# Filler matmuls at the opening, mirrored rows by indexed DMA, and a re-ordered plan in a fused long-convolution and FFN kernel

## The chip, the cores and the metric

The kernel runs on one core of one Trainium2 chip. A core has TensorE (PE), VectorE (DVE), ScalarE (ACT), GpSimd (POOL) and SyncE (SP); SP, ACT and POOL also issue DMAs. The metric is the time of one execution on the device in microseconds (us); of several executions the median counts. A profile is taken of one execution. Its span goes from the first to the last instruction.

## The reference

Two halves work on a sequence of S = 2048 rows with D = 640 columns. The first is a long convolution with a gate, the second an FFN with F = 1728.

```python
k_shift = sum over t of k_pad[:, t:t + S, :] * shift_k[:, 3 - t]     # 4 taps
kv = k_shift * v
y = irfft(rfft(kv, 2S) * rfft(ssm_k, 2S))[:S] + kv * ssm_D           # along the rows
h = x + layernorm(x) * y                                             # x is A_q
h2 = h + (silu(g(h) @ w_gate) * (g(h) @ w_up)) @ w_down              # g is layernorm
```

Inputs and output are bf16.

## The kernel before

The sequence is cut into four blocks of 512 rows, a block into four row tiles of 128. The convolution is done blockwise with cosine and sine transforms of length 1024 as matmuls against constant bases: `g_transform(p)` transforms piece p of the convolution's kernel (eight tiles of 128 frequencies, the cosine half "c" and the sine half "s"), `hbuild` adds neighbouring pieces, `front(n)` makes kv of block n, and `x_transform(n)` its transform. `pair(j, p)` multiplies the transform of block j with that of piece p as complex numbers and adds it to the sum of block j + p: these are the DVE's long instructions, 128 x 2560 elements each (L453). `inverse(n)` brings the sum of block n back (L550), `ln` forms layer-norm statistics (ACT at L520 and L521, or `bn_stats` on the DVE at L516, then two tiny POOL instructions, L524 and L525), and `ffn(n)` does gate and up (L618), the product tT = silu(gate) * up (L632) and the down projection (L644), whose result is added to x on the DVE (L652) and stored.

The transforms use a symmetry: the first 256 rows of a block are needed in reversed order. So `front` mirrors two row tiles of kv on PE by a matmul with a reversed identity (L429), and `inverse` yields the even part es and the odd part os of half a block: their sum is the upper row tile (L566, L567), their difference, mirrored on PE by four matmuls (L574), the lower one, which the DVE reads from PSUM (L577). The normalised rows hl (L532) go transposed to hT by a DMA (L582), which the FFN reads.

The order of all work is computed on the host. Each call of `plan.add` gives an engine, an assumed duration, what is read and written, a priority `pr` and an earliest time `t0`. `Plan.order` simulates the engines with these, three times forward and backward (`ROUNDS = 3`), and keeps the best; the instructions are then issued in that order, and each engine executes its own in order. So SP's queue carries all loads of k, v, x, gate and up weights, the transposes and the stores in one fixed sequence, and one that waits holds back all behind it. PSUM has four buffers: psA0 and psA1 for the convolution, psF0 and psF1 for the kernel transforms and the FFN. The down weights wd are loaded by one DMA of 2,080 KB and one of 80 KB; until then the tile wd holds the transposed kernel pieces 0 to 2, and the first transpose passes through the tile tT (`kch`). F = 1728 is 13 chunks of 128 and a last one of 64, so the last pair of matmuls of each down tile has 64 rows. The first block's conv products come from k loaded once (`front_first`, L395, and banded matmuls, L405); w4, the four taps over all partitions, is made by PE and ACT (L347, L349).

Of the kernel before, what the change touches and what calls it, by code (L numbers as in the profile page):

```python
# [16 lines left out]
D = 640  # L17
# [37 lines left out]
class Plan:  # L55
# [3 lines left out]
    def __init__(self, pools):  # L59
        self.ops, self.writer, self.readers = [], {}, {}  # L60
        self.pools, self.held = pools, {}

    def add(self, eng, dur, fn, r=(), w=(), pr=0, acq=None, rel=None, kb=0, after=(), t0=0.0):
# [8 lines left out]
        i = len(self.ops)  # L72
        self.ops.append(dict(eng=eng, dur=dur, fn=fn, deps=deps, pr=pr, acq=acq and acq[0], rel=rel and rel[0], group=(acq or rel or (0, 0))[1], kb=kb, w=list(w), t0=t0))
# [117 lines left out]
ROUNDS = 3  # L191
# [3 lines left out]
MOVE = "add"  # L195
RES, XACT, VEC, TRANS = (), (), True, {2: 28, 3: 28}
# [11 lines left out]
def kernel(  # L208
# [33 lines left out]
    WI_h = nc.inline_tensor(make_basis()[2], name="const_wi")  # L242
    J_h = nc.inline_tensor(make_flip(), name="const_flip")
# [16 lines left out]
    kch = [tT[:, 2560 * i:2560 * (i + 1)].rearrange("p (a b) -> p a b", a=5) for i in range(2)]  # L260
# [21 lines left out]
    junk = tl("junk", [P, D])  # L282
    mhalf = tl("mhalf", [P, 1], FP32)
# [9 lines left out]
    gT = [wd[:, 0:4, :], wd[:, 4:8, :], wd[:, 8:12, :], hT[1][:].rearrange("p a b -> p (a b)").rearrange("p (a b) -> p a b", a=4)]  # L293

# [14 lines left out]

    def load(q, dst, src, w, pr, kb, r=(), dur=0.45, after=(), t0=0.0):  # L310
# [3 lines left out]

    add("POOL", 0.1, lambda: nc.gpsimd.memset(ones[:], 1.0), w=["ones"], pr=-99)
# [4 lines left out]

    def gload(p, pr, q="SP"):
# [5 lines left out]
        for kt in range(4):  # L327
            g = ("F", "T", p, kt)

            def mm(g=g, kt=kt):  # L330
# [6 lines left out]
            add("PE", 0.45, mm, r=["flip", f"kch{p % 2}"] + (["drow"] if p == 0 and kt == 0 else []), w=[g], pr=pr + 50, acq=("F", g))  # L337
            add("ACT", act(D), lambda g=g, kt=kt: nc.scalar.copy(gT[p][:, kt, :], ps(g).rearrange("p a b -> p (a b)")[:, 0:D]),  # L338
                r=[g], w=[f"gT{p}"], pr=pr - 40, rel=("F", g))
# [11 lines left out]
    for t in range(4):  # L351
        wcast(t)

    def g_transform(p, pr):
        for ct in range(NCT):
            g = ("F", "G", p, ct)

            def mm(g=g, ct=ct):
                for kt in range(4):
                    for h in range(2):  # L360
                        nc.tensor.matmul(ps(g)[:, h, 0:NH], WG[:, kt, ct * P:(ct + 1) * P],  # L361
                                         gT[p][:, kt, h * NH:(h + 1) * NH], start=(kt == 0), stop=(kt == 3))
            add("PE", 8 * 0.137, mm, r=["WG0", "WG1", f"gT{p}"], w=[g], pr=pr, acq=("F", g))
            add("ACT", act(D), lambda g=g, ct=ct: nc.scalar.copy(r3(G[p][ct // 4][:, ct % 4, :]), ps(g)[:, :, 0:NH]),  # L364
                r=[g], w=[Gk[p] + "cs"[ct // 4]], pr=pr - 900, rel=("F", g))
# [4 lines left out]

# [358 lines left out]
```

## Time and profile before

| What | Value |
|---|---|
| median of 8 runs | 296.18 us (294.76 to 297.66) |
| the profiled execution | 297.77 us, its span 296.0 us |
| busy PE / DVE / ACT / POOL | 275.7 / 229.8 / 169.7 / 65.8 us |
| first matmul of the first block's conv (L405) | 10.67 us |
| first y of block 0 on the DVE (L566) | 49.15 us |
| last long DVE instruction of block 3 ends | 227.65 us |
| gate and up of block 3 begin | 247.1 us |
| its down projection begins, last add begins | 276.25, 292.39 us |

A line of the page's second part cuts the span into 40 slices of 7.4 us and gives the busy share of each in tenths. In the chain, each row is a start, a length and what ran; the chain is followed back from the last instruction, at each step to what released it. "Busy" of PE is modelled, and matmuls overlap: 379 ns is the length of a 512-column matmul in the records, but they follow one another at 217 ns; those of 320 columns follow at 136 ns.

### The profile page before, as it was taken

The page shows a single profiled execution, that of the slowest core. Times are in us where ns is not written, and L with a number is a line of the kernel's source. Part 1 is how long each engine was busy: PE and PEld are TensorE (multiplying, and loading weights), DVE is VectorE, ACT ScalarE, POOL GpSimd, SP SyncE. Part 2 cuts the span into 40 slices and gives each one's busy share as a digit, 9 for nine tenths or more (in the row PEclk, how much of TensorE's full clock was granted, in tenths as well). Part 3 has the DMA queues.
Part 4 walks back from the last instruction along what each step waited for, and adds up shares of the span by engine and source line. Part 5 has one row for each costly group of instructions (what it writes and reads, how often), then busy time and mean ns, then how long its engine had stood idle before and what let it go on. Part 6 is the DMA issues. An engine that isn't in the chain of part 4 may idle for free.

```text
span 296.0 us, 4391 instructions
## 1 busy us (share of the span) xinstructions
PE 275.7 (93%) x1636; PEld 158.4 (54%) x1651; DVE 229.8 (78%) x301; ACT 169.7 (57%) x323; POOL 65.8 (22%) x70
## 2 busy tenths in 40 slices
PE   3598969999999989999999999999998999999995
PEld 1366646666645534664545555555444665444563
DVE  0649797999999999999999999999999931221211
ACT  5106896798765588104996790169955732555300
POOL 0000163295000046000353174008810210000000
PEclk9999999999999999999999999999999999999999
DMA  7982399607635587943676294163554152654011
GB/s 225 394 276 82 101 205 355 161 3 216 240 89 133 143 267 146 256 145 89 187 238 200 66 194 96 44 200 91 146 124 111 43 121 59 175 143 105 0 46 46
DMA packets 67898, 44.13 MB, mean 149 GB/s; under 512 B 25442, under 2 KB 65955, under 8 KB 67748
## 3 DMA queue, kind: packets, MB, share of 16 engines
q1 hardware_dynamic: 66240, 40.23, 50.2%
q10 hardware_dynamic: 1636, 3.61, 3.5%
q8 instruction: 13, 0.21, 0.3%
q14 instruction: 9, 0.07, 0.1%
HBM read 37.28 MB, written 2.62 MB: 135 GB/s over the span
## 4 chain that ended last, share of the span: by engine, by line
DVE 51%; PE 31%; DMA 7%; issue 4%; ACT 2%; POOL 2%; ACTq 0%; SPq 0%; DVEq 0%
DVE s L453 20%; DVE T L453 13%; PE psF L644 11%; PE psF L618 11%; DVE k L378 3%; DVE tT L632 3%; PE psA L405 3%; DMA perm<-const_flip 3%; DMA wu<-in_B_w_up_dram 2%; PE psF L361 2%; DVE k L379 2%; PE psA L550 2%; PE psA L443 2%; DMA hT<-hl 1%; DVE o L652 1%
## 5 line engine op out<-in xcount | busy, mean ns | idle before, releaser
L618 PE MATMUL psF<-hT,wg 128*128 128x512 bf16 x273 | 69.0, 379 | 1.3 <-ACT uc L630 0.8
L524 POOL TENSOR_SCALAR sm<-sm 128x1 f32<-128x1 f32 x32 | 30.3, 946 | 171.1 <-ACT junk L521 160.6
L644 PE MATMUL psF<-wd,tT 128*128 128x320 bf16 x448 | 64.8, 299 | 0.5 <-DVE tT L632 0.4
L618 PE MATMUL psF<-hT,wu 128*128 128x512 bf16 x252 | 63.0, 379 | 1.3 <-DMA wu<-in_B_w_up_dram 0.9
L623 ACT ACTIVATE sg<-psF 128x512 bf16<-128x512 f32 (+1 forms) x56 | 33.7, 602 | 45.0 <-PE psF L618 35.8
L644 PEld LDWEIGHTS <-tT 128*128 128x128 bf16 x448 | 41.4, 97 | 23.5 <-issue 6.9
L453 DVE TENSOR_TENSOR T<-s,s 128x2560 bf16<-128x2560 bf16 x32 | 47.4, 1485 | 0.0
L453 DVE TENSOR_TENSOR s<-s,T 128x2560 bf16<-128x2560 bf16 x32 | 47.2, 1484 | 0.0
L618 PEld LDWEIGHTS <-wg 128*128 128x128 bf16 x280 | 27.2, 98 | 32.7 <-issue 2.3
L630 ACT CAST uc<-psF 128x512 bf16<-128x512 f32 (+1 forms) x56 | 33.2, 592 | 16.3 <-PE psF L618 16.1
L632 DVE TENSOR_TENSOR tT<-sg,uc 128x512 bf16<-128x512 bf16 (+1 forms) x56 | 23.5, 423 | 24.3 <-ACT uc L630 24.3
L618 PEld LDWEIGHTS <-wu 128*128 128x128 bf16 x260 | 25.4, 98 | 30.1 <-DMA wu<-in_B_w_up_dram 1.4
L525 POOL TENSOR_TENSOR sm<-sm,mhalf 128x1 f32<-128x1 f32 x32 | 35.1, 1098 | 2.7
L361 PEld LDWEIGHTS <-s 128*128 128x128 bf16 x256 | 25.0, 98 | 11.8 <-issue 2.1
L361 PE MATMUL psF<-wd,s 128*128 128x320 bf16 x192 | 28.4, 299 | 0.9 <-ACT wd L338 0.5
L652 DVE TENSOR_TENSOR o<-psF,x 128x640 bf16<-128x640 f32 x16 | 13.1, 816 | 19.3 <-PE psF L644 19.3
L364 ACT CAST s<-psF 128x640 bf16<-128x640 f32 x32 | 21.8, 693 | 7.7 <-PE psF L361 7.6
L521 ACT ACTIVATE junk<-x,sm 128x640 bf16<-128x640 bf16 x28 | 23.7, 847 | 0.3
L520 ACT ACTIVATE junk<-x 128x640 bf16<-128x640 bf16 x28 | 20.9, 746 | 3.7 <-DVE x L578 2.9
L550 PE MATMUL psA<-s,WI 128*128 128x320 bf16 x128 | 18.9, 299 | 2.9 <-DVE s L453 2.8
L453 DVE TENSOR_TENSOR s<-s,s 128x2560 bf16<-128x2560 bf16 x14 | 20.5, 1482 | 1.2 <-ACT s L364 1.2
L443 PE MATMUL psA<-kv,WX 128*128 128x320 bf16 x128 | 20.5, 299 | 0.0
(55 smaller groups left out, 234.0 us busy)
## 6 DMA issues: line engine op xcount, KB each, us to landing
k<-in_A_k_dram SPq DMA_DIRECT2D x12, 640.0 KB, 4.9
wg<-in_B_w_gate_dram SPq DMA_DIRECT2D x24, 320.0 KB, 3.2
wu<-in_B_w_up_dram SPq DMA_DIRECT2D x24, 320.0 KB, 3.7
out_dram<-o SPq DMA_DIRECT2D x16, 160.0 KB, 1.9
wd<-in_B_w_down_dram SPq DMA_DIRECT2D x1, 2080.0 KB, 10.6
v<-in_A_v_dram SPq DMA_DIRECT2D x12, 160.0 KB, 4.7
x<-in_A_q_dram SPq DMA_DIRECT2D x3, 640.0 KB, 5.4
tT<-in_A_ssm_k_dram SPq DMA_DIRECT2D x2, 640.0 KB, 8.7
```

What stands on the lines that cost most here:

```text
L361: nc.tensor.matmul(ps(g)[:, h, 0:NH], WG[:, kt, ct * P:(ct + 1) * P], gT[p][:, kt, h * NH:(h + 1) * NH], start=(kt == 0), stop=(kt == 3))
L443: nc.tensor.matmul(ps(g)[:, h, 0:NH], WX[:, kt, ct * P:(ct + 1) * P], kv[:, base + kt, h * NH:(h + 1) * NH], start=(kt == 0), stop=(kt == 1))
L453: add("DVE", dve(n * D), lambda: f(o, a, b), r=ks(ak) + ks(bk), w=ks(ok), after=["WG0", "WG1"] if ok[:2] == "s7" else [], pr=pr)
L521: add("ACT", act(D) + 0.45, lambda: nc.scalar.activation(junk[:], src, ACT.Square, bias=s[:, 0:1], accum_out=s[:, 1:2]), r=[xk, k + "a"], ...
L524: e.tensor_scalar(s[:, 3:4], s[:, 1:2], 1.0 if vec else 1.0 / D, EPS, op0=ALU.mult, op1=ALU.add)
L525: e.tensor_tensor(s[:, 4:5], s[:, 3:4], mhalf[:], op=ALU.pow)
L550: nc.tensor.matmul(ps(g)[:, h, 0:NH], WI[:, 4 * part + ct, m * P:(m + 1) * P], a[part][:, ct, h * NH:(h + 1) * NH], start=(ct == 0), stop= ...
L618: i = nc.tensor.matmul(ps(gr)[:, which, :], w[:, kt, cc * P:(cc + 1) * P], hT[b][:, kt, :], start=(kt == 0), stop=(kt == 4))
L623: apart(gr, 0, nc.scalar.activation(sg[s][:z, :], ps(gr)[:z, 0, :], ACT.Silu))
L630: add("ACT", act(MB), lambda gr=gr, s=s, z=z, merged=merged: nc.scalar.copy(uc[s][:z, :], ps(gr)[64:128, 0, :] if merged else ps(gr)[:, 1, ...
L632: add("DVE", dve(MB), lambda c=c, s=s, z=z: TM(tT[:z, c * MB:(c + 1) * MB], sg[s][:z, :], uc[s][:z, :]), r=[f"sg{s}", f"uc{s}"], w=[f"tT{c ...
L644: nc.tensor.matmul(ps(gr)[:, h, 0:NH], tT[:z, c * MB + m * P:c * MB + (m + 1) * P], wd[:z, c, h * NH:(h + 1) * NH], start=(c == 0 and n no ...
```

## The change

- *Fillers.* A tile `junk` is zeroed by the DVE, and PE multiplies it with itself: five matmuls of 512 columns at the start and seven after the broadcast of the taps. The results are not used; a one-element DVE copy after each group releases the PSUM buffer.
- *Zero-padded last chunk.* The lower 64 rows of the last chunk of tT and wd are zeroed once, and the last pair of down matmuls has 128 rows.
- *Down weights.* Four loads (chunks 0 to 3, 4 to 7, 8 to 11, 12) and the one of 80 KB are placed among the gate and up loads of block 0.
- *Mirrored rows.* The lower row tiles 0 and 1 of each x block are gathered row by row in reversed order by an indirect DMA that POOL issues, are kept reversed throughout, and are scattered back to their places by an indirect DMA from POOL at the end. The difference es - os is then formed by the DVE from SBUF, and the L574 matmuls are gone. kv is still mirrored on PE.
- *Transposes.* In blocks 0 and 3 hl is transposed by PE and copied by ACT instead of by DMA (`TURN`).
- *Residual.* In block 2 x is added by two more matmuls per down tile with the identity, and ACT copies the result (`RES`).
- *Statistics.* Row tiles 2 and 3 of block 3 get `bn_stats` on the DVE; block 0 has them for all four as before (`VEC`).
- *Plan.* Named stages get offsets to their priorities (`URGENCY`) and earliest times (`EARLIEST`); the plan is one forward pass (`ROUNDS = 0`). The second buffer of `kch` lies elsewhere in tT, and `hbuild` stands at other places. The order of every engine changes.

```diff
+        i, pr = len(self.ops), pr + URGENCY.get(self.stage, 0)
+        t0 = max(t0, EARLIEST.get(self.stage, 0))
...
-ROUNDS = 3
+URGENCY = {"down 0": 4045, "front 3": -988, "front_first 2": 435, "front_first 3": 3649, "front_tile 3 0": -700, "g_transform 2": 562,
...
+EARLIEST = {"front 2": 89, "front_tile 1 1": 22, "front_tile 2 3": 96, "front_tile 3 0": 153, "g_transform 1": 34, "g_transform 2": 42,
...
+ROUNDS = 0
-MOVE = "add"
-RES, XACT, VEC, TRANS = (), (), True, {2: 28, 3: 28}
+RES = (2,)
+VEC = [(0, q) for q in range(4)] + [(3, 2), (3, 3)]
+TURN = (0, 3)
+GATHER = True
+WARM = (0.3, 5, 7)
...
+    rows = MB * np.arange(NB)[None, :, None] + P * np.arange(2)[None, None, :] + P - 1 - np.arange(P)[:, None, None]
+    idx_h = nc.inline_tensor(np.ascontiguousarray(rows.reshape(P, 2 * NB), dtype=np.int32), name="const_idx")
...
-    kch = [tT[:, 2560 * i:2560 * (i + 1)].rearrange("p (a b) -> p a b", a=5) for i in range(2)]
+    kch = [t.rearrange("p (a b) -> p a b", a=5) for t in (tT[:, 0:2560], tT[:, 8 * MB:13 * MB])]
...
+    add("DVE", 0.35, lambda: nc.vector.memset(junk[:], 0.0), w=["junk"], pr=-999)
+    add("DVE", 0.35, lambda: nc.vector.memset(tT[64:128, 13 * MB:], 0.0), w=["tz"], pr=-998)
+    add("DVE", 0.35, lambda: nc.vector.memset(wd[64:128, 13, :], 0.0), w=["wz"], pr=-998)
+    def warm(name, n, pr, r=()):
+        g = ("F", name)
+        def mm():
+            for i in range(n):
+                nc.tensor.matmul(ps(g)[:, i % 2, :], junk[:, 0:P], junk[:, 0:MB], start=True, stop=True)
+        add("PE", n * WARM[0], mm, r=["junk", *r], w=[g], pr=pr, acq=("F", g))
+        add("DVE", 0.1, lambda: nc.vector.tensor_copy(junk[0:1, 0:1], ps(g)[0:1, 0, 0:1]), r=[g], w=["junk"], pr=pr, rel=("F", g))
+    if WARM[1]:
+        warm("a", WARM[1], -300)
...
+    if WARM[2]:
+        warm("b", WARM[2], -70, r=[("A", "w", 3)])
...
+    def mirror(n, q):
+        return bass.IndirectOffsetOnAxis(ap=idx[:, 2 * n + q:2 * n + q + 1], axis=0)
...
+            load(queue, x[:, 2:4, :], xq[n * MB + 256:(n + 1) * MB, :].rearrange("(m p) d -> p m d", p=P), [f"x{n % 2}_{q}" for q in (2, 3)], pr, 320, t0=(14, 30, 0, 0)[n])
+            for q in (1, 0):
+                add("POOL", 1.2, lambda q=q: nc.gpsimd.indirect_dma_start(out=x[:, q, :], out_offset=None, in_=xq[:, :], in_offset=mirror(n, q), bounds_check=S_TOT - 1,
+                                                                      oob_is_err=False), r=["idx"], w=[f"x{n % 2}_{q}"], pr=pr, kb=160, t0=(14, 30, 0, 0)[n])
...
-                if half == 0:
-                    add("DVE", dve(D), lambda m=m, yb=yb: TA(yb[:], es[m][:], os_[m][:]), r=[f"eo0{m}", f"eo1{m}"], w=[yk], pr=pr)
+                if half == 0 or GATHER:
+                    add("DVE", dve(D), lambda m=m, yb=yb, f=(TA, TS)[half]: f(yb[:], es[m][:], os_[m][:]), r=[f"eo0{m}", f"eo1{m}"], w=[yk], pr=pr)
...
+                if n in TURN:
+                    g = ("A", "Q", n, q)
+                    def mm(g=g, half=half):
+                        flat = ps(g).rearrange("p a b -> p (a b)")
+                        for c in range(5):
+                            nc.tensor.matmul(flat[:, c * P:(c + 1) * P], hl[half][:, c * P:(c + 1) * P], ident, start=True, stop=True)
+                    add("PE", 0.5, mm, r=["flip", hk], w=[g], pr=pr, acq=("A", g))
...
-                        z = 64 if c == 13 else P
                         for h in range(2):
-                            nc.tensor.matmul(ps(gr)[:, h, 0:NH], tT[:z, c * MB + m * P:c * MB + (m + 1) * P],
-                                             wd[:z, c, h * NH:(h + 1) * NH], start=(c == 0 and n not in RES), stop=(c == 13))
+                            nc.tensor.matmul(ps(gr)[:, h, 0:NH], tT[:, c * MB + m * P:c * MB + (m + 1) * P],
+                                             wd[:, c, h * NH:(h + 1) * NH], start=(c == 0 and n not in RES), stop=(c == 13))
...
+            if m < 2 and GATHER:
+                add("POOL", 1.2, lambda m=m, s=s: nc.gpsimd.indirect_dma_start(out=oo[:, :], out_offset=mirror(n, m), in_=ot[s][:], in_offset=None), r=["idx", f"o{s}"], pr=pr - 300, kb=160)
+            else:
+                load("SP", oo[r0:r0 + P, :], ot[s][:], [], pr - 300, 160, r=[f"o{s}"])
...
+    wds = [(0, 4), (4, 8), (8, 12), (12, 13)]
+    def down_loads():
+        for i, (c0, c1) in enumerate(wds):
+            load("SP", wd[:, c0:c1, :], B_w_down[c0 * P:c1 * P, :].rearrange("(kt p) d -> p kt d", p=P), [f"wd{i}"], 1200, 160 * (c1 - c0),
+                 r=[f"tT{2 * min(i, 2) + 1}"], after=["gT0", "gT1", "gT2"])
...
-    load("SP", wd[:, 0:13, :], B_w_down[0:13 * P, :].rearrange("(kt p) d -> p kt d", p=P), ["wdl"], 1200, 2080, after=["gT0", "gT1", "gT2"], t0=40)
```

## The prediction

> **What bounds the kernel now.** I read the page's busy shares, then the chain of work that ended last in order of time (start, duration, what), then busy time by stage, then the timeline at the places that the change touches.
>
> ```profile
> PE 275.7 (93%) x1636; PEld 158.4 (54%) x1651; DVE 229.8 (78%) x301; ACT 169.7 (57%) x323; POOL 65.8 (22%) x70
> DVE  0649797999999999999999999999999931221211
> ```
>
> ```profile
> 10.67 2.31 PE psA L405 x8
> 12.98 1.07 PE psF L413 x4
> 14.05 4.99 PE psA L405 x28
> 20.53 2.01 PE psA L405 x14
> ...
> 49.15 0.50 DVE y L566
> ...
> 227.79 2.35 PE psA L550 x16
> 230.14 0.54 PE psA L574 x4
> 230.68 1.09 PE psF L644 x8
> 231.77 0.54 PE psA L574 x4
> 232.31 14.86 PE psF L644 x104
> 247.54 10.74 PE psF L618 x49
> ```
>
> Stages (stretch; its length; busy us of PE, PEld, DVE, ACT, POOL; clock; DMA share; GB/s):
>
> ```profile
> 60.00:225.00 165.00, 160.62 (x918) 89.23 (x928) 164.01 (x198) 106.01 (x210) 51.48 (x42) 1.00 0.57 152
> 227.75:247.10 19.35, 19.31 (x137) 12.64 (x137) 11.00 (x23) 9.56 (x20) 2.99 (x8) 1.00 0.38 94
> ```
>
> The shares name PE, but there are three stages. Up to 25 us loads and PE set the pace. From 60 to 225 us the DVE works 164.0 of 165.0 us: it is the bound. Its last sum for block 3 ends at 227.65 us (call this E). From there PE works alone: 19.45 us of inverse, mirroring and block 2's down projection until block 3's FFN starts at 247.1, then 29.15 us of gate and up, 16.1 of down, 3.6 of last add and store. A gain must come from E or from these 68.3 us. The profiled execution took 297.77 us, its span 296.0; the median shown is 1.6 us under it. I work out a difference within the span and take it from 296.18.
>
> **The change part by part.**
>
> *Fillers.* By the chain, L405 comes at 289 ns, L413 at 268, and at 20.53 L405 at 144, although the granted clock reads 1.00; the slow stretch lasts from 10.67 to about 15.4. Twelve fillers of 512 columns go ahead, five at the start and seven after the broadcast of the taps. At twice the warm 217 ns of L618 they take 2.2 and 3.0 us. The taps' matmuls end at 6.8; one more load issue (0.35) ahead of ACT's table load, and the first fillers, move that to about 7.5, so fillers run until 10.5. The first product, 0.6 later than now, is ready at 9.7; the 0.8 us between lies before today's 10.67. The slow stretch falls on fillers, and PE wins some 2.5 us. The new order spends them on earlier transposes of the first kernel chunk; the conv result that the DVE waits for at 22.58 comes at the same time. Bounds: 2.5 gained, 1 lost if the fillers run late.
> The Trainium skill, "TensorE: Matmul & The Clock Gate", Part 1, says that about 3.4 us of sustained work lifts the array from half to full rate; the row shows about 4.7. By 3.4 the opening would gain 0.6 us more.
>
> *Reordering.* The DVE now stands 1.72 us before the y at 49.15, waiting for the inverse. After, three conv steps (1.40 + 0.74 + 0.40) stand there and the first inverse's two parts are adjacent on PE. Against that, half of the first kernel transform comes later on PE, behind twenty transposes. I take -1.5 us; bounds -4 and +1. From there to E both kernels have the same 2560-element multiplies and sums of 1.40 us (94 in all before E), so the middle can't shrink.
>
> *Mirrored rows.* PE loses 32 L574 matmuls (0.54 per four, 4.4 us). On the DVE six PSUM reads of 0.73 before E become twelve ops of 0.40: +0.4. Other queues: SP loses eight stores, half of each x load and the eight transposes of blocks 0 and 3, which go to PE and ACT under other work. POOL, in order, gets eight gathers and eight stores, and SP's store of row tile 2 now waits for POOL's two to land. Behind it on SP stand an x load and weights; four chunks (about 11 us of PE with the x transform between) are loaded by then. On POOL the next block's statistics stand behind: they have 25 us in block 0 and 12.6 in block 1, against 3g + 4.
> This g, a DMA issued by POOL, no row shows. I bound it by SP's issue, 0.33 to 0.45 us, and POOL's longest instruction:
>
> ```profile
> 200.78 5.97 POOL L524 TENSOR_SCALAR sm<-sm 128x1 f32<-128x1 f32 x1 [19.71 <-ACT junk L521]
> 233.87 0.19 POOL L524 TENSOR_SCALAR sm<-sm 128x1 f32<-128x1 f32 x1 [18.29 <-ACT junk L521]
> ```
>
> The same instruction takes 0.19 us beside an idle DVE and up to 5.97 beside a full one. The means, 0.95 (L524) and 1.10 (L525), add to 2.0; I take g = 2.0, as an issue is several accesses like those. Where it hurts: row tile 0's output buffer is reused for tile 2, tile 1's for tile 3. In block 0 the new DVE order has 9.2 us of other work between the adds of tiles 1 and 2, and POOL needs two gathers, a store and its landing (1.9, the output row): 3g + 1.9. In block 1 it is 2g + 1.9 against 6.5 for tile 3. Both fit up to g = 2.3. At g = 3 the DVE loses 1.7 + 1.4 = 3.1 us, at 4, 8.1, at 6, 18. I add 0.5.
> The Trainium skill, "SBUF — State Buffer", under "SBUF: two separate sides", speaks against this part: descriptor writing by POOL is locked out by the DVE's two-port modes, 620 ns becoming 3100. No row here shows it; as an estimate, g = 3.1 would cost 3.6 us and put the forecast 3 us higher. The page's "Who interferes with whom" would spare tensor_tensor, by inference.
>
> *Down projection ahead of the inverse.* E is about 227.65 - 1.5 + 0.4 + 0.5 = 227.1. The new PE order puts 48 of block 2's 120 down matmuls (eight of them the new residual) and half of block 3's inverse before the last sum. From the last add of block 1 to E the DVE has 25 x 1.40 + 14 x 0.335 + 3.0 = 42.8 us; PE has 135 x 0.217 + 96 x 0.136 = 42.3 and starts about 1 us earlier. It fits, barely.
> After E: 8 down and 8 inverse matmuls, the os copy, at E + 2.55 the y (now E + 2.2); 13 DVE ops of 0.36 to 0.40, E + 7.65; statistics of tile 2 on the DVE (1.05), a scale, a sum, statistics of tile 3 (1.05), E + 10.5. Meanwhile tile 0's statistics on ACT (1.95) and POOL (0.85), E + 12.5; its scale 0.45, PE transpose 0.2 + 0.44 (the row of L334), ACT copy 0.2 + 0.69: the FFN starts at E + 14.8. PE's own work is 88 x 0.136 + 4 x 0.44 = 13.7, so the chain decides. Now it is E + 19.45: -4.7 us. Without the 48, PE needs E + 20.2: +0.8. The cover of the statistics gets 6.5 us thinner; what is late next is tile 0's.
>
> *Zero padding.* The switch to 64 rows leaves a gap in the weight loads, and so does the switch back:
>
> ```profile
> 238.70 0.11 PEld L644 LDWEIGHTS <-tT 64*128 64x128 bf16 x2 [0.26 <-issue]
> 239.07 3.37 PEld L644 LDWEIGHTS <-tT 128*128 128x128 bf16 x26 [0.26 <-issue]
> ```
>
> Twenty-eight take 4.01 us from 235.06 to 239.07, and 3.80 at 0.136. Four tiles in the last block: -0.9; the other twelve lie under the DVE. The memsets fall in the DVE's first 7.58 idle us.
>
> *Down weights.* One load of 2,080 KB becomes four beside the gate and up loads. A wait of PE for wu (0.94 at 110.74) can go, but the DVE was all but full: 0, bounds -0.4 (the DVE's idle there) and 0.
>
> Sum: -1.5 + 0.4 + 0.5 - 4.7 - 0.9 = -6.2 us; 290.0.
>
> **Rivals.**
> 1. *PE is not ahead at E* (a late weight load, or psF held by a late DVE op). For it: PE is busy 43.6 of 45 us from 180 to 225. Against: at full rate its work from 25 to 227.75 is 405 x 0.217 + 756 x 0.136 + 1.8 = 192.5 of 202.7 us, and about 198 after. The tail is 5.4 us longer: 295.4, no change.
> 2. *POOL's issues hold the output buffers.* In blocks 0 and 1 the DVE waits before an output add. Slower begins where the stalls reach 8.2 us, g = 4.0; g = 5 costs 13.1: 302.6. For it: POOL ops of 2.4, 3.5 and 5.97 us. Against: 36 of 64 take under 0.8.
> 3. *The opening gains all it can*: -4 in place of -1.5, no stall: 287.0.
>
> **How the numbers follow.** Forecast 0.53 (own range 287.5 to 293.0, from -4 to +1 at the opening and g up to 3); rival 1 0.16; rival 2 0.15; rival 3 0.16. A measurement of this kernel can tell about 0.5%, 1.5 us: under 294.7 is faster, over 297.7 slower. The forecast, rival 3 and a quarter of rival 1 are faster, 0.73; the rest of rival 1 is 0.10 the same and 0.02 slower, with rival 2 0.17. The range takes in rivals 1 and 3 and the first part of rival 2: 285.5 to 298.5.
>
> **What would show it.** Right: matmuls at 0.14 us by 12 us; the first y of block 0 near 47; E near 227; block 3's FFN some 15 us after E, with PE idle 1 to 2 us before it; no 64-row gaps; POOL issues near 2 us. Wrong: the DVE idle before an output add, ended by a DMA (rival 2), or gate and up matmuls of block 2 after E (rival 1). The weakest step is E: the order of 300 DVE instructions is redone, and any that waits for PE or ACT adds its wait whole.

## The result and the profile after

The changed kernel takes 298.1 us in the median of 20 executions (296.86 to 303.89), beside 297.04 us of the kernel before (294.76 to 300.11). The ratio is 1.0057, with a 95% interval from 1.0036 to 1.0079: slower by about half a per cent, where the prediction said 290.0 us and a chance of 0.17 for slower. The times of the changed kernel spread widely, and the profiled execution, at 302.82 us and a span of 301.0, is one of the long ones; ratios leave out executions more than 1.5% above the fastest of their kernel, so some of its long ones are not in them (below, three of eight are out in e5 and three of twelve in e14, which lowers those ratios).

From the page of the changed kernel, the span, the busy shares, and the rows by slices of 7.5 us (busy tenths of DVE and POOL, granted clock of PE):

```profile
span 301.0 us, 4515 instructions
## 1 busy us (share of the span) xinstructions
PE 278.2 (92%) x1664; PEld 162.0 (54%) x1679; DVE 230.8 (77%) x316; ACT 177.2 (59%) x327; POOL 114.5 (38%) x86
...
DVE  1757899999999999939999999878999792121221
...
POOL 0220580679997025964500458823000532000020
PEclk9999999999999999998999999959999999999999
```

The DVE's work has hardly changed (230.8 us, before 229.8), but its row is no longer a row of nines: it drops to 3 in one slice, 128 to 135 us, and to 8, 7 and 8 from 188 to 211. POOL's busy time went from 65.8 to 114.5 us. PE idled there too, and its clock row drops just after the first place and inside the second. Busy time by stage shows how much (stretch; its length; busy us of PE, PEld, DVE, ACT, POOL; clock; DMA share; GB/s):

```profile
125.00:135.00 10.00, 5.12 (x36) 3.45 (x34) 5.45 (x5) 4.37 (x9) 7.49 (x3) 0.96 0.21 59
...
190.00:205.00 15.00, 11.34 (x39) 4.42 (x38) 11.04 (x15) 8.46 (x19) 6.64 (x7) 0.77 0.39 112
205.00:235.00 30.00, 29.84 (x167) 16.40 (x168) 29.97 (x31) 17.78 (x31) 3.77 (x3) 1.00 0.47 121
```

Of the 25 us in the first two stretches the DVE works 16.5 and stands 8.5. After both, PE is granted a lower clock (0.77 over the second stretch). The third row is what the rest of the middle looks like: 29.97 of 30.

Both ends of the kernel came as predicted. The chain of work that ended last, at the opening and from the last long sum of block 3 (which ends at 238.28 us, E in the prediction) to the end:

```profile
6.97 3.10 PE psF L351 x7
...
10.78 1.42 PE psA L456 x8
...
13.97 2.01 PE psA L456 x14
```

```profile
239.73 0.70 ACT os L623
...
240.46 0.89 DVE y L635 x2
...
252.55 0.38 PE psF L700
...
281.84 15.23 PE psF L728 x112
...
297.10 0.82 DVE o L736
```

At 13.97 us fourteen matmuls take 2.01 us, 144 ns each; the kernel before took 3.29 us for the fourteen from 13.85 and came to that speed at about 17. The first y after E starts at E + 2.2, block 3's FFN at E + 14.3 (predicted 14.8, before 19.4), its down projection takes 15.23 us in place of 15.96, and E to the end is 62.7 us, predicted 62.8. Everything that is missing lies between the first y of block 0, at 46.07 us, and E: 192.2 us, which before were 178.6. In e5 and e13 below, the same program profiled at 297.33 and 296.60 us, the stretch takes 186.3 and 185.5 us.

What stands in there is read from the timelines of three engines. POOL, then ACT, then the DVE (start, length, engine, line, operation, what it writes and reads, and in brackets the idle time before it and its cause):

```profile
120.71 3.16 POOL L601 DMA_INDIRECT x<-in_A_q_dram,idx  x1 [2.01 <-DVE o L736]
124.18 6.32 POOL L601 DMA_INDIRECT x<-in_A_q_dram,idx  x1 [0.30 <-issue]
130.81 1.01 POOL L739 DMA_INDIRECT out_dram<-o,idx  x1 [0.30 <-issue]
```

```profile
132.56 0.74 ACT L576 ACTIVATE junk<-x 128x640 bf16<-128x640 bf16 x1 [5.63 <-DMA x<-in_A_q_dram,idx]
...
133.29 1.26 ACT L501 CAST s<-psA 128x640 bf16<-128x640 f32 x2
...
187.75 0.74 ACT L576 ACTIVATE junk<-x 128x640 bf16<-128x640 bf16 x1 [8.57 <-DMA x<-in_A_q_dram,idx]
...
193.83 0.74 ACT L576 ACTIVATE junk<-x 128x640 bf16<-128x640 bf16 x1 [4.29 <-DMA x<-in_A_q_dram,idx]
...
195.52 0.57 ACT L705 ACTIVATE sg<-psF 128x512 bf16<-128x512 f32 x1
```

```profile
133.43 0.82 DVE L736 TENSOR_TENSOR o<-psF,x 128x640 bf16<-128x640 f32 x1 [3.81 <-DMA out_dram<-o,idx]
136.20 0.82 DVE L736 TENSOR_TENSOR o<-psF,x 128x640 bf16<-128x640 f32 x1 [1.94 <-PE psA L496]
...
196.60 0.42 DVE L714 TENSOR_TENSOR tT<-sg,uc 128x512 bf16<-128x512 bf16 x1 [2.32 <-ACT uc L712]
```

POOL issues the two gathers of block 2 at 120.71 and 124.18; the second takes 6.32 us and ends only after the DVE has stopped. ACT has the statistics of the gathered tile next in its queue, waits 5.63 us, and only then does the copies of the x transform (L501) that stand behind. The DVE waits 3.81 us ahead of an output add, as POOL comes to the stores of the output buffers only after its gathers, and 1.94 more for PE. At the next block boundary ACT waits 8.57 and 4.29 us for two gathers, and behind them stand the silu and the copy of block 2's FFN (L705, L712); the DVE then waits 2.32 us for the copy, and twice more as PE is slow after its pause. In sum the DVE's waits between the first y and E (those over 0.15 us) are 11.6 us, before 0.9.

### The profile page after: what moved, and what is told of

The parts are those of the page before. It is cut to its first block, busy times and chain, and to the rows that moved or that the text cites. A ratio compares the mean times of both kernels' runs of the same rounds, so it can differ in the third digit from the quotient of the medians.

```text
span 301.0 us, 4515 instructions
## 1 busy us (share of the span) xinstructions
PE 278.2 (92%) x1664; PEld 162.0 (54%) x1679; DVE 230.8 (77%) x316; ACT 177.2 (59%) x327; POOL 114.5 (38%) x86
## 3 DMA queue, kind: packets, MB, share of 16 engines
q10 hardware_dynamic: 1524, 3.29, 2.9%
## 4 chain that ended last, share of the span: by engine, by line
PE 54%; DVE 19%; DMA 8%; ACT 7%; POOL 5%; issue 5%; ACTq 1%; POOLq 0%; DVEq 0%
PE psF L700 31%; PE psF L728 7%; DVE s L506 5%; PE psA L496 5%; DMA x<-in_A_q_dram,idx 5%; PE psF L407 3%; POOL sm L580 3%; PE psA L619 3%; PE psA L456 2%; DMA wg<-in_B_w_gate_dram 2%; DVE T L506 2%; DVE k L424 2%; DMA out_dram<-o,idx 2%; DVE y L635 2%; DVE y L636 1%
## 5 line engine op out<-in xcount | busy, mean ns | idle before, releaser
L700 PE MATMUL psF<-hT,wg 128*128 128x512 bf16 x269 | 71.0, 390 | 6.6 <-ACT uc L712 3.2
L700 PE MATMUL psF<-hT,wu 128*128 128x512 bf16 x256 | 64.9, 384 | 0.3
L580 POOL TENSOR_SCALAR sm<-sm 128x1 f32<-128x1 f32 x32 | 26.1, 816 | 86.0 <-ACT junk L577 72.2
L581 POOL TENSOR_TENSOR sm<-sm,mhalf 128x1 f32<-128x1 f32 x32 | 54.0, 1686 | 2.7
L728 PEld LDWEIGHTS <-tT 128*128 128x128 bf16 x448 | 43.7, 98 | 17.3 <-issue 0.3
L705 ACT ACTIVATE sg<-psF 128x512 bf16<-128x512 f32 (+1 forms) x56 | 33.4, 596 | 23.1 <-PE psF L700 23.1
L712 ACT CAST uc<-psF 128x512 bf16<-128x512 f32 (+1 forms) x56 | 32.7, 584 | 21.5 <-PE psF L700 21.3
L739 POOL DMA_INDIRECT out_dram<-o,idx x8 | 14.2, 1770 | 72.2 <-DVE o L736 39.4
L576 ACT ACTIVATE junk<-x 128x640 bf16<-128x640 bf16 x26 | 19.3, 741 | 22.3 <-DMA x<-in_A_q_dram,idx 18.5
L601 POOL DMA_INDIRECT x<-in_A_q_dram,idx x8 | 19.8, 2481 | 15.8 <-DMA idx<-const_idx 12.1
L736 DVE TENSOR_TENSOR o<-psF,x 128x640 bf16<-128x640 f32 x12 | 9.8, 819 | 16.8 <-PE psF L728 11.1
L577 ACT ACTIVATE junk<-x,sm 128x640 bf16<-128x640 bf16 x26 | 21.6, 832 | 0.3
```

The source lines that it names most:

```text
L577: add("ACT", act(D) + 0.45, lambda: nc.scalar.activation(junk[:], src, ACT.Square, bias=s[:, 0:1], accum_out=s[:, 1:2]), r=[xk, k + "a"], ...
L580: e.tensor_scalar(s[:, 3:4], s[:, 1:2], 1.0 if vec else 1.0 / D, EPS, op0=ALU.mult, op1=ALU.add)
L581: e.tensor_tensor(s[:, 4:5], s[:, 3:4], mhalf[:], op=ALU.pow)
L700: i = nc.tensor.matmul(ps(gr)[:, which, :], w[:, kt, cc * P:(cc + 1) * P], hT[b][:, kt, :], start=(kt == 0), stop=(kt == 4))
L705: apart(gr, 0, nc.scalar.activation(sg[s][:z, :], ps(gr)[:z, 0, :], ACT.Silu))
L712: add("ACT", act(MB), lambda gr=gr, s=s, z=z, merged=merged: nc.scalar.copy(uc[s][:z, :], ps(gr)[64:128, 0, :] if merged else ps(gr)[:, 1, ...
```

## The experiments

The theories that the expectations name: *A*, the DVE, PE and the output stand behind what POOL does late (gathers, stores, statistics), above all through ACT, which executes the gathered tiles' statistics in order ahead of other copies; *B*, rival 2 of the prediction, only the output buffers count; *C*, the new order and the split down weights lose the time, and the indexed DMAs nothing. Numbers of a profile are those of one execution; "idle" is the sum of the DVE's waits over 0.15 us between the first y of block 0 and E.

| Kernel | first y | idle | E | E to end | median us (executions) | ratio to before, 95% |
|---|---|---|---|---|---|---|
| before | 49.15 | 0.9 | 227.7 | 68.3 | 297.04 (57) | |
| changed, as first profiled | 46.07 | 11.6 | 238.3 | 62.7 | 298.1 (20) | 1.0057 [1.0036, 1.0079] |
| e1 no indexed DMAs, re-planned | 46.98 | 6.0 | 232.0 | 69.3 | 303.35 (4) | 1.0266 [1.0216, 1.0316] |
| e2 statistics later | 45.88 | 4.2 | 230.7 | 62.8 | 295.86 (10) | 1.0003 [0.9969, 1.0037] |
| e3 separate output tiles | 45.99 | 4.8 | 231.3 | 62.6 | 296.92 (10) | 1.0025 [0.9985, 1.0065] |
| e4 both | 46.70 | 5.5 | 233.0 | 62.7 | 296.00 (10) | 0.9996 [0.9963, 1.0029] |
| e5 changed again | 46.53 | 5.8 | 232.8 | 62.8 | 297.13 (8) | 0.9940 [0.9903, 0.9977] |
| e6 plain DMAs by SP | 45.71 | 5.3 | 231.4 | 62.6 | 295.92 (10) | 0.9966 [0.9933, 0.9999] |
| e7 no fillers | 46.99 | 6.8 | 234.5 | 62.8 | 299.37 (10) | 1.0070 [1.0034, 1.0107] |
| e8 before, fillers and padding | 49.03 | 1.2 | 228.0 | 66.7 | 295.12 (4) | 0.9885 [0.9820, 0.9950] |
| e9 f32 additions | 46.52 | 4.1 | 234.5 | 62.7 | 299.80 (10) | 1.0116 [1.0084, 1.0148] |
| e10 later, fewer additions | 46.55 | 3.6 | 232.5 | 62.7 | 296.77 (10) | 0.9973 [0.9948, 0.9999] |
| e11 re-planned with prices | 45.32 | 14.0 | 241.0 | 64.6 | 303.05 (8) | 1.0206 [1.0162, 1.0249] |
| e12 before, padding | 46.81 | 0.9 | 225.6 | 66.7 | 295.85 (12) | 1.0002 [0.9976, 1.0029] |
| e13 changed again | 46.69 | 4.9 | 232.2 | 62.6 | 298.26 (12) | 1.0077 [1.0044, 1.0109] |
| e14 statistics later again | 46.26 | 4.0 | 231.0 | 62.8 | 297.29 (12) | 1.0018 [0.9983, 1.0053] |
| e15 before, block 3 gathered | 47.37 | 3.2 | 228.7 | 66.8 | 298.61 (12) | 1.0094 [1.0066, 1.0123] |
| e16 before, fillers and padding | 45.49 | 0.9 | 224.2 | 66.7 | 294.01 (9) | 0.9945 [0.9912, 0.9977] |
| e17 as e9, in bf16 | 46.26 | 4.2 | 233.7 | 62.7 | 298.11 (1) | |

Groups that ran together: e1 to e4, e5 to e8, e9 and e10, e11 to e14, e15 and e16; e17 is a single execution. The medians of before in these groups lie between 295.63 and 297.35, so medians are compared inside a group only, and across groups the ratios.

### No indexed DMAs (e1)

```diff
-GATHER = True
+GATHER = False
```

> The changed kernel with its indexed DMAs alone undone: x is loaded by SP, both stores go by SP, the difference is mirrored on PE again; the plan is made anew for it. Theory A (ACT, in order, waits with the gathered tiles' statistics and holds back the x transform's copies and the FFN's silu behind them) and rival B (the DVE waits for the output buffers that POOL has not stored) both expect the DVE's 12 us of idle time between the first y of block 0 and its last long sum to shrink to 1 or 2, and 288 to 292 us. Rival C (the re-made order and the split down weights lose the time, not the indexed DMAs) expects 296 to 300 us and the idle time to stay. Mind that the host's plan itself sees four more PE steps here, so a loss of up to 2 us on PE at the tail is its own.

It took 303.35 us, beyond what any theory expected, and it can't decide: the plan came out otherwise. PE has the mirrors again, E to the end is 69.3 us, and block 3's FFN starts at E + 21.3. One thing is to be kept: without any indexed DMA the DVE still idles 6.0 us, 5.3 of it ahead of xln and hl, for POOL's statistics (L581).

### Statistics later, separate output tiles, and both (e2, e3, e4)

e2 moves thirteen operations of the finished plan, by number (operation, operation that it is put ahead of): for each gathered tile of blocks 2 and 3 two of ACT and one of POOL, and one scale.

```diff
     seq = plan.order()
+    for i, before in LATE:
+        seq.remove(i)
+        seq.insert(seq.index(before), i)
```

e3 leaves the order alone.

```diff
             s = m % 2
+            o = es[s] if n < 2 and m >= 2 else ot[s]
-            ... ot[s] in the add and in the stores
+            ... o
```

> The changed kernel with nothing moved but the layer-norm statistics of the gathered tiles of blocks 2 and 3: on ACT they stand one at a time among the FFN's copies some 10 to 20 us later, still ahead of their use. Theory A expects the waits of ACT for the gather (5.6, 8.6 and 4.3 us) to vanish, with them the stall at the boundary of blocks 1 and 2 (about 4 to 7 us) and part of the first; 290 to 294 us. Rival B expects the first stall to stay whole (3.8 and 1.9 us ahead of the output adds) and 296 to 298 us. Rival C expects 297 to 299 us.

> The changed kernel with the same order, but the output tiles 2 and 3 of blocks 0 and 1 are written to es0 and es1, which nothing uses then, so that no output add waits for a store of POOL. Rival B expects all of the idle time but some 2 us to go: 288 to 292 us. Theory A expects the wait of 3.8 us to go, but ACT to wait for the gathers as before, and the DVE and PE to stand a little later for ACT instead: 295 to 298 us. Rival C: 297 to 299 us.

> Both edits together: the gathered tiles' statistics later on ACT, and separate output tiles. Theory A, with the output buffers as its smaller part, expects DVE idle time of 1 to 3 us between the first y of block 0 and the last long sum, that sum's end near 228, and 287 to 290 us, which is the prediction's sum. Rival B expects what separate output tiles alone give. Rival C expects 297 to 299 us.

In e2 ACT waits for no gather any more, and the DVE's longest wait is 0.72 us. Idle is 4.2 us, and the ratio 1.0003 after 1.0057: the direction is theory A's, but 295.86 us lies beyond its range of 290 to 294. e3 took the waits for output buffers away and left 1.95 us behind ACT's copy; with 296.92 us rival B's 288 to 292 is refuted, and theory A's 295 to 298 met. e4 should then have reached 287 to 290, and it did not: 296.00, idle 5.5. Most of what is left, 2.9 us in e2 and 4.4 in e4, is the DVE waiting for POOL's statistics. From e2, POOL's timeline and the DVE's:

```profile
72.53 36.40 POOL L582 TENSOR_SCALAR sm<-sm 128x1 f32<-128x1 f32 x1 [4.36 <-ACT junk L579]
109.01 0.55 POOL L583 TENSOR_TENSOR sm<-sm,mhalf 128x1 f32<-128x1 f32 x1
```

```profile
109.59 0.45 DVE L590 TENSOR_SCALAR xln<-x,sm 128x640 bf16<-128x640 bf16 x1 [0.72 <-POOL sm L583]
```

The first is a tensor_scalar on 128 single numbers; the same instruction takes 0.19 us beside an idle DVE. It lasts 36.40 us and ends when the DVE stops, at 108.87, to wait for it. The DVE waits 0.72 us, about the 0.55 of the instruction after it. In the profiles of the changed kernel again (e5) and of e6 and e7 a tiny instruction lasted 41.39 or 41.40 us in the same place, in that of e3 36.39, and in the first profile 24.95. The kernel before had its last statistics of that stretch done at 73.4 us and asked POOL for nothing until 106.92; in the new order the last one, asked for between 68 and 73 us, no longer gets in before the DVE's unbroken row of bf16 instructions begins.

The Trainium skill, "SBUF — State Buffer", section "SBUF: two separate sides", says that POOL and the DVE share a port pair as an exclusive lock, held for the whole instruction, and that the DVE also needs it for two SBUF inputs when POOL reads SBUF. The traces agree that POOL is shut out, and mostly for as long as the page says. In the first profile of the changed kernel, right behind the instruction of 24.95 us (POOL, then the DVE):

```profile
94.75 1.68 POOL L581 TENSOR_TENSOR sm<-sm,mhalf 128x1 f32<-128x1 f32 x1
```

```profile
94.53 1.49 DVE L506 TENSOR_TENSOR T<-s,s 128x2560 bf16<-128x2560 bf16 x1
95.93 0.42 DVE L714 TENSOR_TENSOR tT<-sg,uc 128x512 bf16<-128x512 bf16 x1
96.27 1.49 DVE L506 TENSOR_TENSOR s<-s,T 128x2560 bf16<-128x2560 bf16 x1
```

The DVE doesn't pause, and POOL is through as soon as the DVE goes on to its next instructions. In this profile 16 tiny POOL instructions began beside such a DVE instruction with at least three more of the kind, without a wait, behind it: 14 were done within 1.70 us, before the third of them began; two took 3.12 and 4.00 us (the one of 24.95 us began beside a tensor_scalar and is not counted). Over all nineteen profiles 218 of 264 were done before the third. In the other cases POOL stays out longer, in e2 for a row of some forty instructions of 1.48 us at most. What decides between the two is not shown.

### The changed kernel again, plain DMAs, no fillers (e5, e6, e7), fillers and padding alone (e8)

e6 keeps the order and takes the sixteen indexed DMAs from POOL, so that these rows are not reversed; e7 keeps the order and shrinks the fillers.

```diff
-nc.gpsimd.indirect_dma_start(out=x[:, q, :], ..., in_=xq[:, :], in_offset=mirror(n, q), ...)
+nc.sync.dma_start(out=x[:, q, :], in_=xq[n * MB + q * P:n * MB + (q + 1) * P, :])
...
-            for i in range(n):
-                nc.tensor.matmul(ps(g)[:, i % 2, :], junk[:, 0:P], junk[:, 0:MB], start=True, stop=True)
+            nc.tensor.matmul(ps(g)[0:1, 0, 0:1], junk[:, 0:1], junk[:, 0:1], start=True, stop=True)
```

> The changed kernel as it is, run beside the others of this group so that they can be compared on one chip. 296.5 to 299 us. Theory A as the first four runs left it (POOL gets into SBUF only where the DVE pauses, so everything that POOL does, gathers, stores and statistics alike, comes late, and whatever is queued behind it waits) expects 5 to 12 us of DVE idle time between the first y of block 0 and the last long sum, which begins ahead of the second block-2 gather's consumers on ACT.

> The changed kernel with its order and all its instructions, but the sixteen indexed DMAs of POOL are plain loads and stores of the same bytes by SP, with the rows not reversed (the mirroring of these rows is left out, so they come out in the wrong order). Theory A: the waits for gathers and for stored output buffers go, what is left are the 0.7 us waits for POOL's statistics; DVE idle time 2 to 4 us, 293 to 295.5 us. Rival C (order and weights): no change from the changed kernel, 296 to 299 us. A third possibility: SP, in order, now waits with these loads and holds back weights; then PE waits for wg or wu and the time is as before, 296 to 298.

> The changed kernel with the same order, but each of the two groups of fillers is one matmul of one column. The prediction's step says that the slow stretch of PE then falls on the first products again: matmuls of 0.27 to 0.29 us until about 15 us, the first y of block 0 some 1 to 3 us later than 46.0, and the total later by the same, 299 to 301 us. If the DVE waits for loads there anyway, less than 0.5 us and 297 to 299.

> The kernel before with only the fillers and the zero-padded last chunk, and nothing else of the change; its plan is made as before. By the prediction's steps the padding is worth 0.9 us and the fillers 1 to 2 (the DVE stands 1.7 us ahead of the first y): 293 to 295.5 us against 296.5, and no new wait for POOL. If the plan turns out otherwise with the new steps, 296 to 299.

e5 shows that the first profile was a bad case: idle 5.8 us, not 11.6, in the same program. Its second gather of block 2 happened to be issued quickly. e6 is at 295.92 us, 1.2 under e5, with none of ten executions above 297.1, where e5 has three of eight above 300. As far as so few executions tell, the indexed DMAs make the long ones. But the idle time without them is still 5.3 us, and all but 0.5 of it is this (the DVE's waits; total, times, longest):

```profile
DVE xln L588 <- POOL sm L581: 3.7, 3, 1.6
DVE hl L588 <- POOL sm L581: 1.2, 2, 0.7
```

Theory A expected 2 to 4. POOL's statistics alone hold up the DVE by 4.9 us in the new order, so theory C has a part: the order, which asks for statistics without slack.

e7 lost 2.2 us against e5 in the median, inside its range of 299 to 301; the profile gives 0.46 of it at the first y. e8, with four executions, gained 2.2 against its group. Its shorter stretch after E, 66.7 us for 68.3, is the padding (14.29 and 15.38 us of down projection for 15.02 and 16.11). The first y had not moved, and why is seen in the later run of the same kernel (e16).

### Short additions among the DVE's instructions (e9, e10, e17)

```diff
+            if plan.ops[i]["eng"] == "DVE" and 260 < k < 870 and count % 6 == 0:
+                nc.vector.tensor_add(pause[:], pause[:], pause[:])
```

`pause` has 128 x 32 f32 numbers; e10 has e2's order and every tenth instruction; e17 is e9 in bf16.

> The changed kernel with its order, and 32 additions of 128x32 numbers in f32 put among the DVE's instructions between about 70 and 218 us, one after every sixth: they do nothing for the result. In the earlier runs one of POOL's tiny instructions lasted 36 to 41 us, until the DVE waited. Theory A says that it is shut out by the unbroken row of bf16 instructions of the DVE. If a short f32 instruction breaks that row, POOL's longest instruction between 60 and 225 us falls under 8 us, the DVE's waits for POOL and for copies behind gathers fall from 5.8 to 2 to 3 us, and as the additions themselves cost about 0.1 us each, 3 us, the time is 295 to 298 us. If only a wait of the DVE lets POOL in, the 40 us stay, and the time is 299 to 301 us.

> The statistics of the gathered tiles later on ACT, as in the second run, with 19 such additions, one after every tenth instruction of the DVE. Theory A, if short f32 instructions let POOL in: the DVE's idle time from 4.2 to about 2 us, paid for with some 1.9 us of additions, 294 to 296 us. If they do not: 296.5 to 298.5 us.

> The run with 32 short additions again, but in bf16 like the DVE's other instructions, to tell what let POOL in there. If it is the f32 form, POOL's instruction that begins near 68.5 us lasts 36 to 42 us again and the DVE waits 0.7 to 1.4 us for it near 110. If any short instruction does, it ends within 7 us, at the first addition, as it did with f32 (6.0 us, ended 0.5 us after the addition's start).

This shows what ends POOL's long waits. In e9, POOL's tiny instructions in the stretch where one of them had lasted 41 us, and the additions in the DVE's timeline:

```profile
68.54 6.01 POOL L582 TENSOR_TENSOR sm<-sm,mhalf 128x1 f32<-128x1 f32 x1
74.63 6.03 POOL L581 TENSOR_SCALAR sm<-sm 128x1 f32<-128x1 f32 x1
80.74 5.67 POOL L582 TENSOR_TENSOR sm<-sm,mhalf 128x1 f32<-128x1 f32 x1
```

```profile
74.02 0.21 DVE L799 TENSOR_TENSOR pause<-pause 128x32 f32<-128x32 f32 x1
...
80.50 0.20 DVE L799 TENSOR_TENSOR pause<-pause 128x32 f32<-128x32 f32 x1
...
85.90 0.20 DVE L799 TENSOR_TENSOR pause<-pause 128x32 f32<-128x32 f32 x1
```

Each of these three ends 0.2 to 0.5 us after an addition has started, and the next waits for the next addition. In e17 the addition is bf16, and it does the same:

```profile
74.00 6.71 POOL L582 TENSOR_TENSOR sm<-sm,mhalf 128x1 f32<-128x1 f32 x1
```

```profile
80.20 0.17 DVE L799 TENSOR_TENSOR pause<-pause 128x32 bf16<-128x32 bf16 x1
```

So it is not the f32 form: where POOL is shut out by a row of long instructions, a short one lets it in, f32 or bf16. That such a row does not always shut it out was seen at 94.75 us above. As a cure it is poor: in e9 the DVE works 183.9 us between the first y and E in place of 180.6, 3.3 us for the additions, and idle fell only to 4.1. e9 was slower (299.8; expected 295 to 298), and e10, at 296.77 (expected 294 to 296) and 0.9973 of before, is not clear of e2's 1.0003; its idle time is 3.6 us, where 2 was expected.

### POOL priced in the plan (e11), padding alone (e12), the pair once more (e13, e14)

```diff
-                add("POOL", 1.2, lambda q=q: nc.gpsimd.indirect_dma_start(out=x[:, q, :], ...
+                add("POOL", 2.5, lambda q=q: nc.gpsimd.indirect_dma_start(out=x[:, q, :], ...
...
-                add("POOL", 1.2, lambda m=m, s=s: nc.gpsimd.indirect_dma_start(out=oo[:, :], ...
+                add("POOL", 1.8, lambda m=m, s=s: nc.gpsimd.indirect_dma_start(out=oo[:, :], ...
```

> The changed kernel planned anew with POOL's gathers priced at 2.5 us and its stores at 1.8 (the means of the profiled execution) in place of 1.2 each; nothing else. Theory A: the plan now leaves room for the gathers, so ACT's waits for them shrink from 18 us to under 6, and no execution has the long stalls; but the order has to put the work somewhere, so the gain at the tail shrinks too: 294.5 to 298 us, with a narrower spread than the changed kernel. If the price in the plan doesn't matter, as POOL's time on the chip is set by the DVE's pauses and not by a mean, the waits move elsewhere and the time is 297 to 301.

> The kernel before with the zero-padded last chunk alone, without fillers. In the run with both, the first y of block 0 came at 49.03 against 49.15 us, so the fillers should be worth nothing there, and 14.29 and 15.38 us of down projection in place of 15.02 and 16.11 say that padding is worth 1.5 us after the last long sum: a ratio of 0.993 to 0.996 to before. If the fillers mattered, 0.998 to 1.000.

> The changed kernel as it is, in one group with the others. Theory A expects a wide spread, 295 to 303 us, as one gather more or less that waits for a pause of the DVE decides over several us, and a median of 296.5 to 298.5.

> The changed kernel with the statistics of the gathered tiles later on ACT, as in the second run, in one group with the changed kernel. Theory A expects no execution over 299 us, and a median 1 to 2.5 us under that of the changed kernel of this group. Rival C expects the two to agree in median and spread.

e11 is a clear miss of theory A: 303.05 us. In its profile, which is of its longest execution (307.41 us), ACT waited 29.5 us for gathers, 18.5 in the first profile of the changed kernel, and the output adds 6.3 us for stores. The mean price did not make room for the gathers; as the whole order was made anew, no more can be said. In e14 ACT waits for no gather, in e13 for 11.7 us; the medians differ by 1.0 us and idle is 4.0 against 4.9. That is what ACT's queue seems to cost, but with twelve executions of each it is not clear of their spread (294.08 to 302.05 us in e14, 296.37 to 299.92 in e13). And three of twelve executions of e14 were above 300 us, which theory A had excluded; what made them long was not profiled and stays open.

e12 showed no gain in time (1.0002), though in its profile the stretch after E is 1.6 us shorter than before, as in e8. That kernel's medians leave no room for those 1.6 us unless its opening was as much longer on average; this was not settled.

### Two tries at a better version (e15, e16)

e15 is e12 with the gathers and indexed stores in block 3 alone, and those two tiles' statistics moved later as in e2; e16 is e8 unchanged.

> A try at a version that beats both: the kernel before with the zero-padded last chunk, and with reversed rows gathered and stored by POOL in block 3 alone, whose two gathers have some 40 us until their use and whose stores come when the DVE is all but idle; the gathered tiles' statistics stand late on ACT. Eight mirroring matmuls leave the stretch after the last long sum (1.1 us by PE's 0.136 each), no output buffer waits for POOL in the middle. Theory A: DVE idle time in the middle stays at 1 to 2.5 us, the stretch after the last long sum goes from 66.7 to about 65.6 us: 293 to 295.5 us, 0.990 to 0.997 of before. If even two gathers upset the middle: 296 to 299.

> The kernel before with fillers and padding once more, beside the others: four executions of it gave 0.989 of before, and the padding alone twelve of 1.000. If the fillers matter (as a load that lands late leaves PE cold), 0.988 to 0.994 again; if the four were luck, 0.996 to 1.001.

e15 was slower than before, 1.0094. The DVE idled 3.2 us, 2.28 of it at one FFN copy at 204 us, and the stretch after E stayed at 66.8: PE's down projection (L677) ends earlier, but block 3's FFN (L652) then waits for hT, whose DMA SP issues behind a store. From the chain:

```profile
231.12 11.42 PE psF L677 x84
...
243.91 2.57 DMA hT<-hl
...
246.61 3.40 PE psF L652 x15
```

e16 is the version that beats both: 294.01 us, 0.9945 of before, where the changed kernel is at 1.0057. With e12's 1.0002 this makes the fillers worth some 0.6% in the old order. Its opening, and that of e8 (the same program, in an execution where the constant perm landed late):

```profile
6.57 3.17 PE L326 MATMUL psF<-junk 128*128 128x512 bf16 x7
9.53 1.63 PE L424 MATMUL psA<-k,perm 128*128 128x320 bf16 x8
...
11.27 2.06 PE L424 MATMUL psA<-k,perm 128*128 128x320 bf16 x14
```

```profile
6.58 3.17 PE L326 MATMUL psF<-junk 128*128 128x512 bf16 x7
11.01 2.32 PE L424 MATMUL psA<-k,perm 128*128 128x320 bf16 x8 [1.26 <-DMA perm<-const_flip]
...
13.65 3.22 PE L424 MATMUL psA<-k,perm 128*128 128x320 bf16 x14
```

In e16 the first product follows the fillers at once and takes 1.63 us, then 2.06 for fourteen; the first y comes at 45.49. In e8 PE stands 1.26 us between them, the first product takes 2.32 us, 290 ns a matmul, and the first y comes at 49.03. The Trainium skill, "TensorE: Matmul & The Clock Gate", Part 1, counts the warm-up in time of sustained work, some 3.4 us; the fillers' 3.17 us fit it only where nothing separates them from the first product. Without fillers the first y of the old order lay between 46.81 (e12) and 49.15 us (before, as profiled), as perm landed at different times too (the first product starts at 8.95 and 10.67 us), so more than 2 us of a single profile's opening are chance.

## Why the prediction was wrong, step by step

*What bounds the kernel, and the tail: right; the opening: in part by luck.* The tail from E was worked out as 14.8 us to block 3's FFN and came at 14.3; down matmuls without the 64-row gaps save 0.7 us for four tiles (predicted 0.9); PE was ahead at E, so rival 1 fell. The opening was predicted at -1.5 and "the first y of block 0 near 47"; it came at 46.07 and 46.5 to 46.7 in the later profiles. Against the profiled 49.15 that is more than 1.5, but that execution was a late one, by up to 2.3 us: against e12's 46.81 the gain is 0.1 to 0.7 us. So the number was met in part because the profile of before was late. Fillers were said to move nothing for the DVE; e7 says that they are worth about 2 us, 0.5 of which its profile shows at the first y.

*"E is about 227.65 - 1.5 + 0.4 + 0.5 = 227.1": this sum failed.* From the first y to E the prediction allowed 0.9 us more than before, 179.5 us; the three profiles of the changed kernel have 192.2, 186.3 and 185.5 (first, e5, e13), and E came at 238.3, 232.8 and 232.2. Its two terms were too small, +0.4 for more DVE work and +0.5 for waits. The next paragraphs take them one by one.

*"From there to E both kernels have the same 2560-element multiplies and sums of 1.40 us (94 in all before E), so the middle can't shrink": right, but the middle grew.* Apart from its waits the DVE takes 180.5 to 180.6 us from the first y to E in these three profiles, and before 177.7. The prediction had +0.4 for the new y's, which cost 0.3. It left out what the new order moves into this stretch: two tT products, one of 128 and one of 64 rows (0.7), three xln (1.1) and one kv (0.4); the rest is spread over many groups.

*"On POOL the next block's statistics stand behind: they have 25 us in block 0 and 12.6 in block 1, against 3g + 4": this step failed too.* It measured the slack of the gathers by the time at which the DVE needs the statistics. Their first reader is ACT, in whose queue the statistics stand ahead of the x transform's copies and of the FFN's silu. In the first profile the waits that followed from this are most of the 11.6 us. In e5 and e13 they are less, and moving these statistics and nothing else gave 0.9 us of idle time and 1.0 us of the median (e13 against e14), too little to tell from the spread.

*"I take g = 2.0": the size was near, the form wrong.* In the first profile gathers took 2.48 us in the mean and stores 1.77, but one by one from 1.0 to 6.32 us; in e13 the means are 1.28 and 2.08. A price times a count misses this spread, which decides whether there is a stall: the stall of rival 2 was there (3.81 and 1.94 us in the first profile, 0.3 in e5), and e3 took it away without reaching 292.

*No term at all stood for the statistics that were there before.* The prediction used POOL's 0.19 to 5.97 us only to bound g. But the new order asks for a statistic at the start of the DVE's unbroken stretch, and 4.9 us of DVE waits for POOL remain in e6, with no indexed DMA left. Before, such waits were 0.9 us. Why POOL stays out so long there, and is through at once elsewhere beside the same DVE instructions, stays open.

In sum: 2.5 us more of DVE work than predicted; and in the three profiles of the changed kernel (first, e5, e13) 1.4, 2.5 and 3.2 us of waits for POOL's statistics and 10.1, 3.2 and 1.7 of other waits, mostly for gathers, output buffers and what stands behind them, where the prediction had added 0.5 to the 0.9 of before. The 5.6 us won at the tail are given back in the middle.

## What to carry to other kernels

An instruction's slack is measured from the first engine that executes its consumer in order, with all that is queued behind it there, not from the engine that needs the value last. Beside a DVE that never pauses, the duration of a POOL instruction is no one number: most were through within 1.8 us here, some only at the next pause, up to 41 us later. Look where the order puts it and who needs it, not at its mean. And before an opening is priced from one profile, see how far the landing of its first loads wanders.

## What the runs showed of the hardware that was not expected

- A POOL instruction on 128 numbers lasted 21.5 to 41.4 us, in eleven profiles, beside a DVE that executed bf16 tensor_tensor instructions on two SBUF tiles (128 x 512 to 128 x 2560) without a pause, and ended within 0.5 us of the start of a DVE wait; with additions in the row it ended within 0.5 us of the start of one of 0.17 to 0.21 us, f32 or bf16. A DVE wait of 0.16 us was enough (first profile, at 92.79). Most such POOL instructions, 218 of 264, got in at one of the next two DVE instructions without any of this. The Trainium skill, "SBUF — State Buffer", section "Who interferes with whom", names tensor_tensor with two SBUF inputs as contending with POOL's reads, which fits; that POOL is sometimes passed over for a whole row of them is only seen here.
- An indexed DMA of 128 rows of 1,280 bytes was issued in 1.0 us with the DVE idle (130.81 in the first profile), and in 1.5 to 6.3 us at the block boundaries of that profile with the DVE at work. But a full DVE does not always slow it: in e13 the gathers at 122.25 and 123.63 took 1.07 and 1.02 us beside one.
- After PE's two pauses in the first profile (4.9 us idle from 125 to 135, 3.7 from 190 to 205) its granted clock was lower (0.74 from 135 to 140 us, 0.57 and 0.75 from 195 to 205), so such a stall can cost more than its length: two further DVE waits, of 0.78 and 0.87 us, followed the second.
